# Two attention branches on one core: permuting the 16x16 weights instead of the evictions, and 744 instead of 712 score tiles on VectorE

## The chip, the core and the metric

The program runs on one core of one Trainium2 chip. The core has five engines with a queue each: TensorE (PE, matmuls), VectorE (DVE), ScalarE (ACT), GpSimd (POOL) and SyncE (SP, which only issues transfers here). PE writes into PSUM, eight banks of 128 partitions x 512 fp32; DVE and ACT read PSUM and write SBUF; POOL works in SBUF. The metric is the device time of one execution in microseconds, as the median of several runs.

## The reference

With S = 2048 rows, D = 512, H = 32 heads of 16 columns:

```python
def _A_ref(x, wqkv, w_phi, wo):
    q, k, v = ...                       # from x @ wqkv, per head
    pq = jnp.einsum("bhsd,hdf->bhsf", q, w_phi)
    pk = jnp.einsum("bhsd,hdf->bhsf", k, w_phi)
    phi_q = jnp.concatenate([_softmax(pq), _softmax(-pq)], axis=-1)
    phi_k = jnp.concatenate([_softmax(pk), _softmax(-pk)], axis=-1)
    kv, z = ...                         # sums over s of phi_k x v, and of phi_k
    o = num / den                       # phi_q x kv, phi_q x z
    return o.reshape(B, S, D) @ wo
def _B_ref(x, wqkv, wo):
    scores = jnp.einsum("bhqd,bhkd->bhqk", q, k) * (Dh ** -0.5)
    p = _softmax(scores, axis=-1)
    return (p @ v).reshape(B, S, D) @ wo
x = A_x
g = _sigmoid((x * gate_w).sum(-1, keepdims=True))
return g * _A_ref(...) + (1 - g) * _B_ref(...)
```

Branch A is linear attention with a learned feature map; branch B is ordinary softmax attention, and most of the work.

## The kernel before

**Branch B.** A block is one head out of each of four groups and one chunk of 512 queries; there are 32 blocks. A block has 64 score tiles of 128 keys x 512 queries (4 heads x 16 key tiles), 2,048 in all. A score matmul (`qk_mm`, L1290) contracts over 32 rows only, so matmuls of different heads run side by side in the rows of the PE array. Two tiles at a time go to ACT, which makes the exponential of 128 x 1024 from PSUM into `E_t` (L1381). Two such pairs of banks take turns, so the pair j+2 is written when ACT has read pair j. The remaining tiles of a block, `DN[b]` of them, go to DVE through three other banks: DVE adds a constant and writes int16 (L1367; L1357 where two tiles are joined in one instruction of 1,024 columns), which read as bf16 is a coarse exponential. POOL adds a constant to four int16 at a time in int64 words (L1343), into a second buffer and later once more on that buffer, for a group of four tiles; the three versions together approximate the exponential. The products with V (`pv_mm`, L1402) contract over 128 keys and give 32 columns, so four of them run side by side in the columns of the array. An ACT tile needs one product, a DVE tile three. The buffers of the DVE tiles (`Tx`, `Ty`, `Tz`, `oT`, `WoA`, `vA` and more) are borrowed from tensors not needed at the time.

**Branch A.** `Wp` is the projection folded with the 16x16 feature weights: for queries and for keys, `WAT` (the transposed projection) times a block-diagonal matrix `Wbd` of the 16x16 weights. Eight small DMAs on POOL's queue write the blocks of `Wbd` (L1039). `wp_fill` makes the eight products into PSUM (L1624, four matmuls of 128 columns each), and a DVE copy puts each into `Wp` (L1628). That copy also reorders the columns: four heads at a time, from head-major (j, f) to feature-major (f, j), which is a write with stride four. Later stages read `Wp` in that order (`phi`, L1051 for the matmuls).

**Fillers.** Where PE would have little to do, the planner puts matmuls with a tensor of zeros in (L1392).

**What sets the order.** All operations are declared with engine, duration, priority, reads and writes. `Plan.layout` schedules them in a list by modelled durations and gives an order for each engine. `settle` then changes that order by a table, `MOVES`: for each engine pairs (from, to) of places in its queue; `drop`, PE operations (fillers) that are left out; `banks`, another PSUM bank for a fill; `pairs`, two DVE tiles joined in one instruction; `locks`, POOL adds that are made to wait for a DVE operation. Every queue runs in the order that results, with semaphores for the dependencies. `DN` feeds `layout`: it says how many tiles of each block DVE takes, and so how many pairs ACT has.

Of the kernel before, what the change touches and what calls it, by code (L numbers as in the profile page):

```python
# [15 lines left out]
D = 512  # L16
H = 32
DH = 16
KT = 4
# [11 lines left out]
DN = (6, 20, 20, 24, 26, 22, 22, 20, 22, 22, 24, 18, 22, 20, 20, 26, 30, 22, 24, 26, 22, 24, 22, 26, 18, 22, 28, 18, 24, 24, 32, 16)  # L31
# [60 lines left out]
    ),  # L92
    "act": (
# [3 lines left out]
    ),  # L97
# [795 lines left out]
def _build(ctx, nc, A_x, A_wqkv, A_w_phi, A_wo, B_wqkv, B_wo, gate_w, out):  # L893
    names = [0]

    def sb(shape, dt=BF16, name="sb"):
        names[0] += 1
        return ctx.enter_context(nc.sbuf_tensor(f"{name}_t{names[0]}", shape, dt))
# [6 lines left out]
    WAT = sb([128, 8, D], name="WAT")  # L905
# [1022 lines left out]
```

## Time and profile before

| | us |
|---|---|
| runs, median of 3 | 682.58 (682.48 to 683.23) |
| profiled execution, its own time | 682.9 |
| its span, first to last instruction | 680.7 |
| ACT busy in it | 656.2 |
| PE busy in it | 670.5 |
| DVE busy in it | 591.1 |
| POOL busy in it | 383.2 |

The profile is of one execution. Busy is the time in which at least one instruction of the engine ran; a matmul's end is modelled, and neighbouring ones overlap, so PE's 670.5 is more than the time in which it could take no further work. A line of a group gives source line, engine, operation, tiles, shapes and count, then busy time in all, mean ns of one, and the idle time of the engine just before them with what ended it. In the timeline the first two columns are start and duration. In the windows each engine has its busy time and, in brackets, its number of instructions.

### The profile page before, as it was taken

Reading aid. Unit: us, or ns where it says so; the run is one execution under the profiler, and the core shown is the slowest. Engines: PE = TensorE matmul, PEld = TensorE weight load, DVE = VectorE, ACT = ScalarE, POOL = GpSimd, SP = SyncE. Lnnn points to the kernel's source line nnn. Section 1 sums busy time; section 2 is a strip of 40 time slices with the busy share of each in tenths; the row PEclk is TensorE's granted clock in tenths of the full one; section 3 lists DMA queues with packets and bytes.
Section 4 is the critical chain, followed back from the end, with each engine's and each line's share of the span. In section 5 each row is a group of like instructions: output and inputs, shape, how many; then the busy total and the mean of one; then the engine's idle time right before and its main releaser. Section 6 shows DMA issues by size and latency. Waiting matters only on the chain.

```text
span 680.7 us, 20896 instructions
## 1 busy us (share of the span) xinstructions
PE 670.5 (99%) x8995; PEld 232.9 (34%) x8995; DVE 591.1 (87%) x920; ACT 656.2 (96%) x739; POOL 383.2 (56%) x415
## 2 busy tenths in 40 slices
PE   8989999999999999999999999999999999999997
PEld 4322333334233333333233233322332333333333
DVE  4699889878998889898988989899799888989984
ACT  6999999999999999999999999999999999999995
POOL 7045466543666445654666766665656646565853
PEclk9999999999999999999999999999999999999999
DMA  6800100000010000000113022121321324033221
GB/s 132 161 29 10 29 16 15 19 14 19 10 23 15 11 18 11 17 18 14 18 41 87 27 69 72 46 49 48 81 66 34 68 72 99 27 72 82 65 72 39
DMA packets 67467, 30.95 MB, mean 45 GB/s; under 512 B 52696, under 2 KB 62296, under 8 KB 67376
## 3 DMA queue, kind: packets, MB, share of 16 engines
q1 hardware_dynamic: 66368, 28.95, 18.0%
q8 instruction: 70, 1.15, 0.7%
q10 hardware_dynamic: 576, 0.52, 0.2%
q0 software_dynamic: 432, 0.15, 0.1%
q14 instruction: 21, 0.17, 0.1%
HBM read 7.87 MB, written 8.88 MB: 25 GB/s over the span
## 4 chain that ended last, share of the span: by engine, by line
PE 78%; ACT 15%; DVE 5%; DMA 1%; issue 0%
PE psO L1402 28%; PE psS L1290 27%; PE psS L1051 15%; ACT E_t L1381 14%; PE psO L1392 2%; PE psS L1666 2%; DVE Wp_t L1628 1%; PE psS L1763 1%; DMA ld<-Tf_t 1%; PE psS L1142 1%; PE psS L1155 1%; PE psS L1750 1%; DVE Tz_t L1367 1%; DVE Ty_t L1357 1%; PE psS L1005 0%; DVE Tx_t L1367 0%
## 5 line engine op out<-in xcount | busy, mean ns | idle before, releaser
L1381 ACT ACTIVATE E_t<-psS 128x1024 bf16<-128x1024 f32 x668 | 625.2, 1054 | 12.9 <-PE psS L1290 11.6
L1290 PE MATMUL psS<-qz_t,kTB_t 32*128 32x512 bf16 x2048 | 275.4, 384 | 4.2 <-DVE Wp_t L1628 1.5
L1367 DVE TENSOR_SCALAR Tx_t<-psS 128x512 int16<-128x512 f32 x232 | 154.4, 685 | 15.5 <-PE psS L1290 14.0
L1290 PEld LDWEIGHTS psS<-qz_t,kTB_t 32*128 32x128 bf16 x2048 | 71.9, 91 | 236.3 <-ACT E_t L1381 114.6
L1402 PE MATMUL psO<-E_t,vaug_t 128*32 128x512 bf16 (+1 forms) x1336 | 109.4, 383 | 0.0
L1343 POOL INT64_ADD vA_t<-vA_t x69 | 68.0, 992 | 26.0 <-PE psO L1402 24.5
L1367 DVE TENSOR_SCALAR Ty_t<-psS 128x512 int16<-128x512 f32 x106 | 71.3, 684 | 8.8 <-PE psS L1290 7.6
L1402 PE MATMUL psO<-vA_t,vaug_t 128*32 128x512 bf16 x494 | 48.0, 383 | 0.0
L1367 DVE TENSOR_SCALAR oT_t<-psS 128x512 int16<-128x512 f32 x60 | 40.5, 683 | 5.5 <-PE psS L1290 4.9
L1367 DVE TENSOR_SCALAR Tz_t<-psS 128x512 int16<-128x512 f32 x58 | 39.0, 685 | 6.3 <-PE psS L1290 6.0
L1343 POOL INT64_ADD Ty_t<-Ty_t x39 | 39.8, 1019 | 7.5 <-PE psO L1402 7.4
L1343 POOL INT64_ADD Ty_t<-Tx_t x28 | 28.3, 1010 | 26.5 <-DVE Tx_t L1367 13.9
L1402 PE MATMUL psO<-Ty_t,vaug_t 128*32 128x512 bf16 (+1 forms) x414 | 41.6, 384 | 0.0
L1343 POOL INT64_ADD phiQT_t<-Tx_t x18 | 17.9, 992 | 41.0 <-DVE Tx_t L1367 34.6
L1367 DVE TENSOR_SCALAR vA_t<-psS 128x512 int16<-128x512 f32 x52 | 35.0, 684 | 6.3 <-PE psS L1290 6.3
L1402 PEld LDWEIGHTS psO<-E_t,vaug_t 128*32 128x32 bf16 (+1 forms) x1336 | 27.3, 95 | 38.2 <-issue 27.1
L1051 PE MATMUL psS<-xT_t,WB_t 128*32 128x512 bf16 x464 | 38.0, 383 | 0.1
L1051 PE MATMUL psS<-Wp_t,xT_t 128*32 128x512 bf16 x512 | 37.8, 382 | 0.0
L1367 DVE TENSOR_SCALAR WAT_t<-psS 128x512 int16<-128x512 f32 x50 | 33.5, 682 | 3.0 <-PE psS L1290 2.7
L1343 POOL INT64_ADD vA_t<-Tx_t x20 | 19.9, 998 | 25.8 <-DVE Tx_t L1367 24.6
L1367 DVE TENSOR_SCALAR Wp_t<-psS 128x512 int16<-128x512 f32 x46 | 31.0, 684 | 2.4 <-PE psS L1290 1.8
L1392 PE MATMUL psO<-xT_t,zero_t 128*32 128x512 bf16 x328 | 32.0, 385 | 0.0
(165 smaller groups left out, 914.3 us busy)
## 6 DMA issues: line engine op xcount, KB each, us to landing
dpq<-EA_t SPq DMA_DIRECT2D x16, 256.0 KB, 2.1
Rb_t<-lr SPq DMA_DIRECT2D x120, 32.0 KB, 1.8
dpo<-kv_t SPq DMA_DIRECT2D x16, 128.0 KB, 1.8
qz_t<-qz_t SPq DMA_DIRECT2D x120, 16.0 KB, 1.8
Tf_t<-Tf_t SPq DMA_DIRECT2D x60, 32.0 KB, 2.0
WB_t<-in_B_wqkv_dram SPq DMA_DIRECT2D x3, 384.0 KB, 4.4
out_dram<-WvA_t SPq DMA_DIRECT2D x8, 128.0 KB, 1.9
out_dram<-WB_t SPq DMA_DIRECT2D x6, 128.0 KB, 1.9
```

The costliest lines, as they stand in the source:

```text
L1051: ins = e.matmul(out[32 * i:32 * i + 32, :], lhsT=lhsT[:, 32 * i:32 * i + 32], rhs=rhs, start=start, stop=stop, tile_position=(0, 32 * i))
L1142: mms = [lambda e, ap, i=i, t=t: e.matmul(ap[:, 128 * i:128 * (i + 1)], lhsT=xT[:, t, NQ * c + 128 * i:NQ * c + 128 * (i + 1)], rhs=W_B[:, ...
L1155: mms = [lambda e, ap, i=i, t=t: e.matmul(ap[:, 256 * i:256 * (i + 1)], lhsT=xT[:, t, NQ * c + 128 * (2 * hf + i):NQ * c + 128 * (2 * hf + ...
L1290: return e.matmul(bank, lhsT=kT_B[32 * i:32 * i + 32, ROW[b // 2] % 2, 128 * kt:128 * (kt + 1)], rhs=qz[32 * i:32 * i + 32, b // 2 % 4, b ...
L1343: op = P.add("pool", P64 + W64 * size, d_prio(g["ts"][0]) - 5.0 + (0.0 if key == "s" else M_LATE), lambda e: e.int64_add(words(dst), words ...
L1357: return e.tensor_scalar(dst[:, a[0]:a[1] + 1:a[1] - a[0], :].bitcast(I16), src[:, b[0]:b[1] + 1:b[1] - b[0], :], EXPB, 0.0, op0=ALU.add, ...
L1367: ops.append(drain(f, mm, "dve", 0.70, d_prio(d), lambda e, ap, q=q: e.tensor_scalar(quarter(tb, q).bitcast(I16), ap, EXPB, 0.0, op0=ALU.a ...
L1381: op = P.add("act", EXP_OVH + 0.4267 * n, 0.0, lambda e: e.activation(Ebuf[:, j // 2 % EPAIRS, 512 * SZ[0] * (j % 2):512 * SZ[0] * (j % 2) ...
L1392: ins = e.matmul((psO if bank is None else bank)[32 * i:32 * i + 32, :], lhsT=zero[:], rhs=xT[:, 0, 0:NQ], start=bank is not None, stop=ba ...
L1402: return e.matmul(psO[32 * i:32 * i + w, :], lhsT=vaug[:, kt, o:o + w], rhs=rhs, start=start, stop=stop, tile_position=(0, 32 * i), skip_g ...
L1628: wp_ops.append(drain(f, mm, "dve", 0.69, prio, lambda e, ap: e.tensor_copy(Wp[:, t, D * qk:D * (qk + 1)].rearrange("p (a f j) -> p a j f" ...
L1666: mms = [lambda e, ap, n=n, f=f: e.matmul(ap[:, 64 * n:64 * n + 64].rearrange("p (s g j) -> p s g j", s=2, j=4), lhsT=ident[:], rhs=es[n][ ...
```

## The change

A second tensor `Wbp` holds the block-diagonal weights with their columns already in the feature-major order. One copy on POOL makes it from `Wbd` once the eight DMAs have landed. The products of `wp_fill` use `Wbp`, and the DVE copy behind them becomes plain. In six blocks more tiles go to DVE: four more in blocks 5, 6, 12 and 13, eight more in blocks 22 and 26.

```diff
-DN = (6, 20, 20, 24, 26, 22, 22, 20, 22, 22, 24, 18, 22, 20, 20, 26, 30, 22, 24, 26, 22, 24, 22, 26, 18, 22, 28, 18, 24, 24, 32, 16)
+DN = (6, 20, 20, 24, 26, 26, 26, 20, 22, 22, 24, 18, 26, 24, 20, 26, 30, 22, 24, 26, 22, 24, 30, 26, 18, 22, 36, 18, 24, 24, 32, 16)
...
 MOVES = {
...
     Wbd = sb([128, KT, 128], name="Wbd")
+    Wbp = sb([128, KT, 128], name="Wbp")
...
     P.join_writes(wbd_ops, "Wbd")
+    pool(1.0, -3.9, lambda e: e.tensor_copy(Wbp[:].rearrange("p r (a f j) -> p (r a) f j", f=DH, j=4),
+                                            Wbd[:].rearrange("p r (a j f) -> p (r a) f j", j=4, f=DH)),
+         reads=["Wbd"], writes=["Wbp"], name="wbp")
...
     def wp_fill(qk, t, prio):
         mms = [lambda e, ap, r=r: e.matmul(ap[:, 128 * r:128 * (r + 1)], lhsT=WAT[:, 4 * qk + r, 128 * t:128 * (t + 1)],
-                                           rhs=Wbd[:, r, :], start=True, stop=True) for r in range(KT)]
-        f, mm = fill(prio, mms, ["Wbd"] + [("WAT", 4 * qk + r) for r in range(KT)], name=f"W{qk}{t}", chunk=4,
+                                           rhs=Wbp[:, r, :], start=True, stop=True) for r in range(KT)]
+        f, mm = fill(prio, mms, ["Wbp"] + [("WAT", 4 * qk + r) for r in range(KT)], name=f"W{qk}{t}", chunk=4,
                      dur=0.07, cols=128)
-        wp_ops.append(drain(f, mm, "dve", 0.69, prio, lambda e, ap: e.tensor_copy(
-            Wp[:, t, D * qk:D * (qk + 1)].rearrange("p (a f j) -> p a j f", j=4, f=DH), ap.rearrange("p (a j f) -> p a j f", j=4, f=DH)),
+        wp_ops.append(drain(f, mm, "dve", 0.69, prio, lambda e, ap: e.tensor_copy(Wp[:, t, D * qk:D * (qk + 1)], ap),
                             writes=[("Wp", qk, t)], name=f"We{qk}{t}"))
```

The table `MOVES` is another throughout, on every engine. Its lists grow or shrink a little: places moved on PE 1,835 to 1,856, on DVE 569 to 584, on POOL 180 to 191, on SP 101 to 92, on ACT 33 both; banks 581 to 613, locks 187 to 204, joined pairs 54 both, dropped fillers 207 to 201.

Built, the two programs differ in their instructions as follows; everything else has the same count in both, in another order.

| engine | instruction | before | after |
|---|---|---|---|
| ACT | exponential of two tiles into `E_t` | 668 | 652 |
| DVE | score tiles (joined pairs counted twice) | 712 | 744 |
| DVE | strided copy into `Wp` | 8 | 0 |
| DVE | plain copy into `Wp` | 0 | 8 |
| POOL | copy `Wbd` to `Wbp` | 0 | 1 |
| POOL | int64 adds | 374 | 390 |
| PE | products with V from `E_t` | 1,336 | 1,304 |
| PE | products with V from DVE tiles | 2,136 | 2,232 |
| PE | fillers | 364 | 300 |
| PE | all matmuls | 8,995 | 8,995 |

663 rows, old and new, of the table MOVES are left out of this document.

## The prediction

> **What bounds the kernel now.** I read the page's busy times and chain first, then the groups by line, then the timeline of an ordinary stretch, then windows of 20 us for the places where that stretch is not typical.
>
> ```profile
> span 680.7 us, 20896 instructions
> PE 670.5 (99%) x8995; PEld 232.9 (34%) x8995; DVE 591.1 (87%) x920; ACT 656.2 (96%) x739; POOL 383.2 (56%) x415
> PE 78%; ACT 15%; DVE 5%; DMA 1%; issue 0%
> ...
> L1381 ACT ACTIVATE E_t<-psS 128x1024 bf16<-128x1024 f32 x668 | 625.2, 1054 | 12.9 <-PE psS L1290 11.6
> ...
> L1367 DVE TENSOR_SCALAR Tx_t<-psS 128x512 int16<-128x512 f32 x232 | 154.4, 685 | 15.5 <-PE psS L1290 14.0
> ```
>
> Two engines are nearly full at once. An exponential on ACT takes 625.2/668 = 0.936 us of its time, and ACT hardly idles before one (12.9 us in all). The chain of waits, however, runs through PE for 78% of the span. DVE has room, 591.1 of 680.7. A busy PE is not yet a PE at its limit, so the timeline has to say which of the two ends last:
>
> ```profile
> 299.65 6.55 ACT L1381 ACTIVATE E_t<-psS 128x1024 bf16<-128x1024 f32 x7
> ...
> 303.75 0.39 PE L1290 MATMUL psS<-qz_t,kTB_t 32*128 32x512 bf16 x3
> ...
> 304.07 0.40 PE L1402 MATMUL psO<-Tx_t,vaug_t 128*32 128x512 bf16 x4
> ...
> 304.30 0.39 PE L1402 MATMUL psO<-phiQT_t,vaug_t 128*32 128x512 bf16 x4
> ...
> 304.62 0.39 PE L1290 MATMUL psS<-qz_t,kTB_t 32*128 32x512 bf16 x3
> ```
>
> Matmuls on different strips of the array start together, as one pass. After a pass of the same tiling the next starts 0.23 us later (304.07 to 304.30); after a change between row tiling (scores) and column tiling (products with V) it starts 0.32 us later, so a change costs about 0.10 us more. One score pass and two column passes are 0.87 us, against 0.936 us for the exponential: ACT wins here by 0.07 us, and a third column pass would make PE last. Counted in the built program, PE's queue has 1,238 runs of one tiling, with 118 further row passes and 905 further column passes inside them: 1,238 x 0.32 + 1,023 x 0.23 = 631 us, before the short whole-array products. So PE is a second bound close behind ACT. The windows say how often each is last:
>
> ```profile
> 40.00:60.00 20.00, 17.55 (x187) 5.37 (x187) 20.00 (x24) 17.24 (x18) 10.27 (x10) 1.00 0.03 7
> ...
> 120.00:140.00 20.00, 20.00 (x298) 7.78 (x296) 16.27 (x24) 20.00 (x25) 10.20 (x12) 1.00 0.06 16
> ...
> 340.00:360.00 20.00, 19.98 (x299) 7.22 (x295) 17.17 (x30) 18.72 (x22) 12.47 (x13) 1.00 0.11 35
> ...
> 480.00:500.00 20.00, 20.00 (x290) 7.22 (x292) 16.57 (x29) 20.00 (x24) 11.97 (x13) 1.00 0.38 89
> 500.00:520.00 20.00, 19.86 (x264) 6.76 (x256) 19.42 (x32) 20.00 (x24) 13.04 (x14) 1.00 0.12 36
> ...
> 660.00:680.00 20.00, 17.01 (x262) 6.92 (x254) 10.50 (x18) 13.45 (x15) 7.20 (x7) 0.97 0.16 48
> sum 680.00, PE 670.50 PEld 232.91 DVE 591.10 ACT 656.20 POOL 383.21; mean PE 19.72 PEld 6.85 DVE 17.39 ACT 19.30 POOL 11.27
> ```
>
> Columns after the length are PE, PE loads, DVE, ACT, POOL, clock. ACT is busy for 20.00 of 20 in 15 of the 34 windows (as at 120 and 480), and short of it in the rest (as at 340). The window at 40 alone has DVE full and ACT down at 17.24.
>
> **The change part by part.**
>
> *Sixteen exponentials less.* Tiles on DVE go from 712 to 744, so ACT makes 652 exponentials: 16 x 0.936 = 15.0 us less on ACT. That is the gain if ACT ends every stretch.
>
> *PE.* Per tile moved, one product leaves and three come: 96 - 32 = 64 matmuls more; 64 filler matmuls (a product with zeros) go. PE's total stays what it was. Counted by passes: score passes 725 to 723, column passes 1,436 to 1,437, runs 1,238 to 1,203. With the prices above, -1 x 0.23 - 35 x 0.10 = -3.7 us. That is the gain if PE ends every stretch.
>
> I weigh the two by the windows: 15/34 x 15.0 + 19/34 x 3.7 = 8.7 us. Both ends stay for the range.
>
> *The evictions of Wp.* Eight strided writes become plain ones:
>
> ```profile
> L1628 DVE CAST Wp_t<-psS 128x512 bf16<-128x512 f32 x8 | 10.2, 1298 | 0.0
> ...
> L1118 DVE CAST kTB_t<-psS 128x512 bf16<-128x512 f32 x14 | 9.6, 686 | 3.6 <-PE psS L1051 3.4
> ```
>
> ```profile
> L1628 DVE CAST Wp_t<-psS x8: 1278/1296/1325, 39.7 to 57.1; 128x512 bf16<-128x512 f32 x8
> ```
>
> ```profile
> 42.22 0.38 PE L1290 MATMUL psS<-qz_t,kTB_t 32*128 32x512 bf16 x1 [0.72 <-DVE Wp_t L1628]
> ...
> 43.51 1.02 ACT L1381 ACTIVATE E_t<-psS 128x1024 bf16<-128x1024 f32 x1 [0.87 <-PE psS L1290]
> ```
>
> The plain form of the same shape, L1118, takes 0.686 us against 1.298: 8 x 0.61 = 4.9 us off DVE, all between 39.7 and 58.4 us. There it is on the path: the score matmul at 42.22 stands behind an eviction, and the exponential at 43.51 stands behind the matmul. ACT lost 20 - 17.24 = 2.8 us in that window. At most that comes back, at least nothing; since the new order puts further DVE tiles close by, I take 1.0.
>
> *The copy on POOL.* No row has a 128x512 copy; its neighbours are these:
>
> ```profile
> 2.43 2.29 POOL L1030 MEMSET vaug_t<- 128x512 bf16 x1
> ...
> 9.16 4.09 POOL L1039 DMA_DIRECT2D Wbd_t<-in_A_w_phi_dram  x8 [0.17 <-POOL mask_t L1043]
> 13.24 0.25 POOL L1044 COPY mask_t<-mask_t 128x64 bf16<-128x64 bf16 x1
> 30.73 0.61 POOL L1343 INT64_ADD phiQT_t<-Tx_t  x1 [17.24 <-DVE Tx_t L1367]
> ```
>
> ```profile
> L1624 PE MATMUL psS<-Wbd_t,WAT_t x32: 219/219/230, 38.7 to 56.4; 128*128 128x128 bf16 x32
> ...
> DMA to landing us min/median/max: 2.3/2.6/3.6
> ```
>
> A strided fill of that size took 2.29 us, an eighth of the copy 0.25 (times eight, 2.0); from below, the small copy's 0.25 is a floor. I take 2.0. It is a new wait at the head of POOL's queue: eight landings, the last issued by 13.25 and landed by 16.9 at the latest. Queued behind it are the adds, the first at 30.73 after 17.24 us of idleness, and the Wp products on PE from 38.7. That idleness covers it: nothing. With the cover gone it would be 2.0 us on the first add and, through it, on the first products.
>
> *DVE.* Thirty-two tiles at 154.4/232 = 0.666 us are 21.3, less 4.9: 16.4 us more, 607.5 in all. Against a span near 670 that is 91%, so in total it fits. It need not fit in every place. Block 22 and block 26 get eight more tiles each, and in the built order, cut into stretches of 24 exponentials, tiles on DVE per stretch had two values above 31 (33 and 32) and now have five (36, 34, 34, 32, 32). Other DVE work is (591.1 - 712 x 0.666)/28 = 4.2 us a stretch, and a stretch lasts 680.7/668 x 24 = 24.5 us. DVE is over that by 3.7 us at 36 tiles, 2.3 at 34, 1.0 at 32: 10.3 in sum, against 2.7 before. Neighbouring stretches have room, but only three banks hold scores ahead of DVE. Bounds 0 and +7.6; I take half, 3.8.
>
> *POOL.* Sixteen more adds:
>
> ```profile
> L1343 POOL INT64_ADD vA_t<-vA_t x69 | 68.0, 992 | 26.0 <-PE psO L1402 24.5
> ```
>
> ```profile
> L1512 DVE TENSOR_TENSOR oT_t<-Tf_t,Rb_t x15: 627/682/691, 83.9 to 656.2; 128x512 bf16<-128x512 f32 x15
> ```
>
> At 0.99 each that is 15.8 us on an engine that is 56% busy: about 399 + 2 of some 670. It waits mostly for PE to free a buffer, so it is not last: nothing. The order's list also ties 204 adds to a DVE operation instead of 187; such a wait holds POOL's queue alone. SP issues the same 501 transfers in another order: nothing. These two hide behind the same exponentials; uncovered, one add is worth at most its own 1.0 us.
>
> DVE's multiplies with two SBUF inputs (L1512) took at most 0.691 us, no more than a plain eviction, so none of the 15 stood behind an add. The Trainium skill (SBUF — State Buffer, "SBUF: two separate sides") has it that such an operation and a GpSimd instruction that reads SBUF exclude each other for a whole instruction; by that rule 17 more POOL instructions can cost up to 17 us where they meet, and the trace agrees only in that it shows no meeting.
>
> **Sum.** 682.9 is the profiled execution's own time (span 680.7 and 2.2 around it). -8.7 - 1.0 + 3.8 = -5.9: 677.0. That execution is 0.3 above the median of the runs, 682.58, so I forecast **676.7**.
>
> **The rivals.**
>
> *ACT ends everything.* If the new order fits PE's work and DVE's crowded places under the exponentials, the full 15.0 comes, and up to 2.8 in the Wp stretch: 682.6 - 15.0 - 2.0 = 665.6. For it: the cycle at 303.75 has ACT last by 0.07 us. Against it: 19 windows where ACT is not full.
>
> *PE ends everything.* -3.7 + 3.8 leaves 682.6, no change. For it: 631 us of passes and changes, and the chain's 78%. Against it: 300 of 364 filler matmuls are still in the built program, and a stretch with fillers has room on PE.
>
> *DVE takes the bound in the crowded stretches.* There DVE drains the banks late, the next score matmul waits for one, and what stands behind it on PE, ACT's next pair among it, waits too, as at 42.22. ACT's saving is then idle time. Place: the five stretches above; price: the full 7.6, with PE last elsewhere (-3.7) and nothing from Wp: 682.6 + 3.9 = **686.5**, slower. It decides once a stretch holds more than (24.5 - 4.2)/0.666 = 30.5 tiles. For it: the window at 40, where full DVE cost ACT 2.8 us. Against it: the window at 500, where DVE had 19.42 and ACT still 20.00.
>
> *A POOL add meets a two-input DVE operation*, and one of the two stands for 0.99 us. If half of the 17 new POOL instructions did, and PE or ACT stood with it, 8.4 us would be added: 685.1. It is the rule cited above that makes this possible.
>
> *The clock falls.* In the last window PE is at 17.01 of 20 and its clock at 0.97. With 64 fillers gone a stretch might thin out like that; at 0.97 over half the span, 10 us more: 686.7. But the fillers are replaced one for one, in less time. The Trainium skill (TensorE: Matmul & The Clock Gate, "What's actually happening") has the clock fall after an idle window of some 3.4 us; the trace has no such hole in PE before the tail.
>
> *The plain eviction is not plain*, and stays at 1.30 us: the 1.0 and half of the 4.9 are lost, 680.2. L1118 speaks against it.
>
> **How the numbers follow.** Forecast 0.47 (670 to 681); ACT ends everything 0.19; PE ends everything 0.08; DVE crowded 0.19; port 0.03; clock 0.02; eviction not plain 0.02. A difference under about 0.2%, or 1.4 us, can't be told from none here. Faster by more than that: 0.47 + 0.19 + 0.02 = 0.68; within it 0.08; slower 0.24. The range 666 to 688 takes in all bounds but the corners: below it half of the second case lies, above it some of the slower ones.
>
> **What would show it.** ACTIVATE to E_t x652 at an unchanged 0.936 (busy by count), and ACT's idle time before it between 13 and 25 us: right; 30 or more, with waits of the score loads on DVE tiles doubled: DVE crowded. Evictions of Wp near 0.69 us and the window 40 to 60 with ACT above 18.5: that step right. The copy between 16 and 20 us, and no Wp product waiting for it. Granted clock 1.00 outside the tail. The forecast is wrong if ACT's busy time falls by 15 us and the span by less than 2 or by more than 13.

## The result, and the profile after

| | before | after |
|---|---|---|
| median of the runs, us | 682.88 (682.48 to 683.23) | 676.08 (675.27 to 676.94) |
| profiled execution, us | 682.9 | 675.81 |
| its span, us | 680.7 | 673.9 |

The ratio of the times is 0.9901, with an interval of 0.9884 to 0.9918: 6.8 us faster, where 5.9 were forecast. The page of the changed kernel, in lines that answer to those of before (busy times, chain, the exponentials; the second half of the kernel has moved down by 10 or 11 lines):

```profile
PE 665.2 (99%) x8995; PEld 233.7 (35%) x8995; DVE 602.8 (89%) x952; ACT 643.0 (95%) x723; POOL 401.0 (59%) x432
...
PE 81%; DVE 9%; ACT 7%; DMA 1%; issue 1%; SPq 0%; DVEq 0%
...
L1392 ACT ACTIVATE E_t<-psS 128x1024 bf16<-128x1024 f32 x652 | 611.6, 1049 | 20.0 <-PE psS L1301 16.1
```

ACT lost 13.2 us of work (656.2 to 643.0), the span half of that. PE lost 5.3, and ACT's part of the chain went from 15% to 7%. An exponential still takes 0.94 us of ACT (611.6/652).

The first thing to look for is where on the way the 6.8 us appear. From the trace, the time at which the first exponential of a block starts:

| block | tiles added | before | after | difference |
|---|---|---|---|---|
| 1 | 0 | 35.1 | 34.8 | -0.3 |
| 2 | 0 | 58.9 | 55.3 | -3.6 |
| 4 | 0 | 101.2 | 96.5 | -4.7 |
| 7 | 4 each in 5 and 6 | 164.6 | 157.9 | -6.7 |
| 8 | 0 | 185.1 | 179.4 | -5.8 |
| 22 | 8 in it | 471.5 | 464.6 | -6.9 |
| 23 | 0 | 493.1 | 482.7 | -10.4 |
| 24 | 0 | 511.5 | 504.1 | -7.4 |
| 26 | 8 in it | 553.0 | 545.8 | -7.2 |
| 27 | 0 | 571.9 | 562.0 | -9.9 |
| 28 | 0 | 595.2 | 588.6 | -6.6 |
| end | | 680.7 | 673.9 | -6.7 |

At the start of block 5, the first that got more tiles, 5.2 us are there (120.6 to 115.5), three quarters. Blocks 22 and 26, with sixteen of the 32 new tiles, gain some 3 us each while they run, for want of exponentials, and the block behind each gives it back.

The first stretch is that of the `Wp` evictions. The timeline of ACT in it, before and then after (start, duration, what ran; in brackets the idle time ahead and what ended it):

```profile
33.21 9.43 ACT L1381 ACTIVATE E_t<-psS 128x1024 bf16<-128x1024 f32 x10
43.51 1.94 ACT L1381 ACTIVATE E_t<-psS 128x1024 bf16<-128x1024 f32 x2 [0.87 <-PE psS L1290]
45.67 3.27 ACT L1381 ACTIVATE E_t<-psS 128x1024 bf16<-128x1024 f32 x3 [0.22 <-PE psS L1290]
49.13 1.94 ACT L1381 ACTIVATE E_t<-psS 128x1024 bf16<-128x1024 f32 x2 [0.20 <-PE psS L1290]
51.53 4.69 ACT L1381 ACTIVATE E_t<-psS 128x1024 bf16<-128x1024 f32 x5 [0.46 <-PE psS L1290]
56.93 2.98 ACT L1381 ACTIVATE E_t<-psS 128x1024 bf16<-128x1024 f32 x3 [0.71 <-PE psS L1290]
```

```profile
32.97 28.03 ACT L1392 ACTIVATE E_t<-psS 128x1024 bf16<-128x1024 f32 x30
```

Before, 25 exponentials took from 33.21 to 59.91, 1.07 us each. After, 30 of them ran without a break in 28.03, 0.934 each. At that pace 25 take 23.4 us, so 3.3 us were lost before. The gaps add up to only 2.46: the rest lies in the short rows between them, since two exponentials in a row take 1.94, 0.97 each, and 0.93 is only reached in a long row. Records of neighbours overlap there, so a break costs more than the gap that the timeline shows. This is why counting idle time undersells the loss. The evictions and the new copy, in the views by tile and of POOL's timeline:

```profile
L1639 DVE CAST Wp_t<-psS x8: 677/680/692, 35.1 to 51.9; 128x512 bf16<-128x512 f32 x8
```

```profile
L1635 PE MATMUL psS<-Wbp_t,WAT_t x32: 219/219/230, 34.4 to 51.4; 128*128 128x128 bf16 x32
```

```profile
16.97 1.08 POOL L1050 COPY Wbp_t<-Wbd_t 128x512 bf16<-128x512 bf16 x1 [3.52 <-DMA Wbd_t<-in_A_w_phi_dram]
33.23 0.61 POOL L1354 INT64_ADD phiQT_t<-Tx_t  x1 [15.18 <-DVE Tx_t L1378]
```

An eviction is 0.680 us (median of eight). The copy takes 1.08 us behind the landings, POOL then idles for 15.18, and the first product that reads it comes at 34.4: it is hidden. Last, windows of 20 us (PE, PE loads, DVE, ACT, POOL, clock), one in the `Wp` stretch, two in the crowded blocks and the tail:

```profile
40.00:60.00 20.00, 20.00 (x244) 6.28 (x242) 19.45 (x28) 19.91 (x23) 12.33 (x12) 1.00 0.03 7
480.00:500.00 20.00, 19.91 (x300) 7.58 (x300) 19.41 (x35) 17.45 (x22) 13.82 (x14) 1.00 0.25 66
560.00:580.00 20.00, 19.74 (x278) 6.99 (x270) 20.00 (x34) 15.93 (x17) 14.15 (x15) 1.00 0.28 76
660.00:680.00 20.00, 10.49 (x174) 4.66 (x166) 5.86 (x10) 7.11 (x9) 4.14 (x4) 0.93 0.08 27
```

In the first, PE went from 17.55 to 20.00 and ACT from 17.24 to 19.91. In the third, DVE is full and ACT idles for 4 us, as in the first before the change; that looks like DVE as the bound, and the third experiment below tests it.

### The profile page after: what moved, and what is told of

Read it like the earlier page. It is cut to its first block, busy times and chain, and to the rows that moved or that the text cites. A ratio compares the mean times of both kernels' runs of the same rounds, so it can differ in the third digit from the quotient of the medians.

```text
span 673.9 us, 20931 instructions
## 1 busy us (share of the span) xinstructions
PE 665.2 (99%) x8995; PEld 233.7 (35%) x8995; DVE 602.8 (89%) x952; ACT 643.0 (95%) x723; POOL 401.0 (59%) x432
## 4 chain that ended last, share of the span: by engine, by line
PE 81%; DVE 9%; ACT 7%; DMA 1%; issue 1%; SPq 0%; DVEq 0%
PE psS L1301 29%; PE psO L1413 28%; PE psS L1062 14%; ACT E_t L1392 6%; PE psS L1676 3%; DVE Tx_t L1378 2%; PE psO L1403 2%; DVE Ty_t L1378 1%; PE psS L1153 1%; PE psS L1166 1%; DVE WAT_t L1378 1%; DMA ld<-Tf_t 1%; PE psS L1773 1%; DMA Lq_t<-ld 1%; DVE vA_t L1378 1%
## 5 line engine op out<-in xcount | busy, mean ns | idle before, releaser
L1392 ACT ACTIVATE E_t<-psS 128x1024 bf16<-128x1024 f32 x652 | 611.6, 1049 | 20.0 <-PE psS L1301 16.1
L1378 DVE TENSOR_SCALAR Tx_t<-psS 128x512 int16<-128x512 f32 x250 | 164.3, 681 | 13.2 <-PE psS L1301 11.8
L1413 PE MATMUL psO<-E_t,vaug_t 128*32 128x512 bf16 (+1 forms) x1304 | 106.4, 383 | 0.1
L1354 POOL INT64_ADD vA_t<-vA_t x72 | 71.5, 1001 | 35.7 <-PE psO L1413 21.3
L1354 POOL INT64_ADD Ty_t<-Ty_t x42 | 43.3, 1032 | 15.0 <-PE psO L1413 10.2
L1413 PE MATMUL psO<-vA_t,vaug_t 128*32 128x512 bf16 (+1 forms) x520 | 49.9, 383 | 0.0
L1413 PE MATMUL psO<-Ty_t,vaug_t 128*32 128x512 bf16 x436 | 43.9, 383 | 0.0
L1378 DVE TENSOR_SCALAR WAT_t<-psS 128x512 int16<-128x512 f32 x58 | 39.2, 685 | 4.2 <-PE psS L1301 3.8
L1378 DVE TENSOR_SCALAR oT_t<-psS 128x512 int16<-128x512 f32 x56 | 37.4, 683 | 5.1 <-PE psS L1301 4.8
L1413 PEld LDWEIGHTS psO<-E_t,vaug_t 128*32 128x32 bf16 (+1 forms) x1304 | 27.4, 95 | 35.3 <-issue 22.5
L1062 PE MATMUL psS<-Wp_t,xT_t 128*32 128x512 bf16 x512 | 37.7, 382 | 0.0
L1378 DVE TENSOR_SCALAR vA_t<-psS 128x512 int16<-128x512 f32 x52 | 35.1, 683 | 2.4 <-PE psS L1301 1.9
L1062 PE MATMUL psS<-xT_t,WB_t 128*32 128x512 bf16 x464 | 36.6, 383 | 0.0
L1413 PE MATMUL psO<-Tx_t,vaug_t 128*32 128x512 bf16 x282 | 29.7, 387 | 0.0
```

What stands on the lines that cost most here:

```text
L1062: ins = e.matmul(out[32 * i:32 * i + 32, :], lhsT=lhsT[:, 32 * i:32 * i + 32], rhs=rhs, start=start, stop=stop, tile_position=(0, 32 * i))
L1354: op = P.add("pool", P64 + W64 * size, d_prio(g["ts"][0]) - 5.0 + (0.0 if key == "s" else M_LATE), lambda e: e.int64_add(words(dst), words ...
L1378: ops.append(drain(f, mm, "dve", 0.70, d_prio(d), lambda e, ap, q=q: e.tensor_scalar(quarter(tb, q).bitcast(I16), ap, EXPB, 0.0, op0=ALU.a ...
L1392: op = P.add("act", EXP_OVH + 0.4267 * n, 0.0, lambda e: e.activation(Ebuf[:, j // 2 % EPAIRS, 512 * SZ[0] * (j % 2):512 * SZ[0] * (j % 2) ...
L1413: return e.matmul(psO[32 * i:32 * i + w, :], lhsT=vaug[:, kt, o:o + w], rhs=rhs, start=start, stop=stop, tile_position=(0, 32 * i), skip_g ...
```

## The experiments

They begin with the two parts of the change, apart (1, 2). Then DVE is made shorter where it is crowded (3) and where it is not (4), ACT everywhere (5, 6), and PE in its fillers (7). Another home for DVE's work follows (8), then a shorter PE (9, 10), and then two and three engines shorter at once (11, 12). Each was run beside the kernel before; ratios are to that. Differences to the changed kernel are to the 676.08 of the result above, since it wasn't run again; the kernel before came to between 682.84 and 683.02 in these later runs.

**1. The plain evictions alone, in the old order.**

```diff
+    Wbp = sb([128, KT, 128], name="Wbp")
...
-                                           rhs=Wbd[:, r, :], start=True, stop=True) for r in range(KT)]
+                                           rhs=Wbp[:, r, :], start=True, stop=True) for r in range(KT)]
...
-            Wp[:, t, D * qk:D * (qk + 1)].rearrange("p (a f j) -> p a j f", j=4, f=DH), ap.rearrange("p (a j f) -> p a j f", j=4, f=DH)),
+        wp_ops.append(drain(f, mm, "dve", 0.69, prio, lambda e, ap: e.tensor_copy(Wp[:, t, D * qk:D * (qk + 1)], ap),
...
+    q.insert(max(k for k, o in enumerate(q) if o.name.startswith("wbd") or o.name == "mk2") + 1, wbp)
```

> The kernel before with its own order and 712 tiles; only the weights are permuted by the POOL copy and the eight evictions of Wp are plain. Theory A (the plain evictions are worth most of the gain, since DVE was last between 39 and 58 us): 4 to 5 us faster than before, about 678.3; window 40 to 60 with ACT above 19.5. Theory B (the prediction's size for this step, the rest of the early gain being the new order): about 1 us faster, 681.8. Theory C (nothing of it shows in the end, later stretches absorb it): 682.8.

Measured: 678.51 against 682.96, ratio 0.9925 (0.9897 to 0.9952), 4.45 us faster. ACT's timeline of this run:

```profile
33.21 26.95 ACT L1397 ACTIVATE E_t<-psS 128x1024 bf16<-128x1024 f32 x29
```

The order is that of before; only eight evictions and the copy differ, and the gaps are gone: 29 exponentials in 26.95, and ACT is busy for all 20.00 us from 40 to 60. By this run the plain evictions are worth about two thirds of the gain. The run's interval and the changed kernel's overlap, so the other third is not shown by it alone.

**2. The new tiles and the new order, with strided evictions.** The copy stays in, and nothing reads it.

```diff
-                                           rhs=Wbp[:, r, :], start=True, stop=True) for r in range(KT)]
+                                           rhs=Wbd[:, r, :], start=True, stop=True) for r in range(KT)]
...
-        wp_ops.append(drain(f, mm, "dve", 0.69, prio, lambda e, ap: e.tensor_copy(Wp[:, t, D * qk:D * (qk + 1)], ap),
+        wp_ops.append(drain(f, mm, "dve", 0.69, prio, lambda e, ap: e.tensor_copy(
+            Wp[:, t, D * qk:D * (qk + 1)].rearrange("p (a f j) -> p a j f", j=4, f=DH), ap.rearrange("p (a j f) -> p a j f", j=4, f=DH)),
```

> The changed kernel with its new order and 744 tiles; the evictions of Wp are strided again (1.30 us) and the products use the unpermuted weights; the copy on POOL is still made and unused. Theory A: 4 to 5 us slower than the changed kernel, about 680.5, that is 2 us faster than before, which would be the worth of the moved tiles and the new order. Theory B: about 1 us slower, 677.

Measured: 679.4, ratio 0.9951 (0.9929 to 0.9973): 3.3 us above the changed kernel's 676.08, and 3.6 below before. The view by tile and the window at 40:

```profile
L1639 DVE CAST Wp_t<-psS x8: 1285/1317/1342, 35.4 to 55.2; 128x512 bf16<-128x512 f32 x8
```

```profile
40.00:60.00 20.00, 18.34 (x205) 5.63 (x203) 19.98 (x24) 17.80 (x20) 10.50 (x11) 1.00 0.03 8
```

The holes in PE and ACT are back. So the evictions bring 3.3 us (by this run) to 4.45 (by the first), and tiles and order the remaining 2.4 to 3.6.

Tiles and order were not run apart, but the traces divide them in part. Block 5, the first with more tiles, starts at 120.6 before, at 116.7 with the evictions alone, at 119.2 with the order and the tiles alone, and at 115.5 with all. Up to there no tile has moved: the evictions bring 3.8 to 3.9 and the new order 1.3 to 1.4. Of the 6.7 us in the end, 1.5 are left for the 32 tiles and the rest of the order.

The traces can also be cut into stretches of 24 exponentials. In us, from the first exponential of a stretch to the first of the next:

| stretch | before | 1 | after | 2 | 3 |
|---|---|---|---|---|---|
| 1 | 24.7 | 22.0 | 22.3 | 25.6 | 22.4 |
| 2 | 24.1 | 22.8 | 22.2 | 22.5 | 22.2 |
| 7 | 22.2 | 22.2 | 22.2 | 22.2 | 22.2 |
| 19 | 24.0 | 24.0 | 26.6 | 26.7 | 26.4 |
| 22 | 23.0 | 23.0 | 26.1 | 26.2 | 25.9 |
| 23 | 24.1 | 24.2 | 27.0 | 27.0 | 26.8 |

**3. DVE's tiles at half their columns, where DVE is crowded** (stretches 19, 20, 22, 23).

```diff
+            c = 256 if g["n"] in HALF else 512
-            return e.tensor_scalar(dst[:, a[0]:a[1] + 1:a[1] - a[0], :].bitcast(I16), src[:, b[0]:b[1] + 1:b[1] - b[0], :], EXPB, 0.0,
+            return e.tensor_scalar(dst[:, a[0]:a[1] + 1:a[1] - a[0], 0:c].bitcast(I16), src[:, b[0]:b[1] + 1:b[1] - b[0], 0:c], EXPB, 0.0,
...
+        if op.kind == "dq" and (pairs - 1) // 24 in (19, 20, 22, 23):
+            share[op.group] += 1
```

> The changed kernel; about 136 DVE tiles, those whose scores are made between the exponentials 456 to 503 and 528 to 575, are evicted by half (256 of 512 columns), so the output is not the reference's. This takes some 0.3 us each off DVE in the stretches where it was full after the change. Theory D (DVE took the bound there, the gain of the tiles moved into blocks 22 and 26 was lost in it): 4 to 6 us faster than the changed kernel, about 671, and ACT's idle time before the exponentials down from 20 to about 12. Theory P (PE ends these stretches): under 1.5 us faster.

Measured: 676.03, ratio 0.9885 (0.9839 to 0.9932): the changed kernel's time. A window of this run:

```profile
560.00:580.00 20.00, 19.65 (x278) 6.61 (x272) 14.42 (x34) 16.41 (x18) 15.55 (x16) 1.00 0.31 76
```

DVE falls from 20.00 to 14.42 in it, and ACT has only one instruction more in it. The account called D, that DVE is the bound there, falls, although DVE was full and ACT idle.

**4. The same where DVE has room**, by `in (7, 8, 9, 16, 17)` in place of the four stretches of the third.

> The changed kernel; about the same number of DVE tiles (148) are evicted by half, but those of the exponentials 168 to 239 and 384 to 431, where DVE had idle time. Theory D: 0 to 1.5 us faster, since DVE is not last there. If it gains as much as the run with the crowded tiles, DVE matters everywhere alike and crowding is no cause.

Measured: 675.3, ratio 0.9874 (0.9834 to 0.9914), 0.8 below the changed kernel, whose ratio the interval holds. In neither set of stretches does a shorter DVE alone bring a gain that is clear of noise; at the `Wp` evictions, in the first experiment, it did.

**5 and 6. Shorter exponentials**, in the changed kernel and in the kernel before: 960 of 1,024 columns from the 60th on.

```diff
-            Ebuf[:, j // 2 % EPAIRS, 512 * SZ[0] * (j % 2):512 * SZ[0] * (j % 2) + 512 * n], psS[:, 512 * base:512 * (base + n)], ACTF.Exp, scale=ESCALE),
+            Ebuf[:, j // 2 % EPAIRS, 512 * SZ[0] * (j % 2):512 * SZ[0] * (j % 2) + 512 * n - 64 * (j >= 60)],
+            psS[:, 512 * base:512 * (base + n) - 64 * (j >= 60)], ACTF.Exp, scale=ESCALE),
```

> The changed kernel; every exponential from the 60th on makes 960 of its 1,024 columns (592 of them, some 0.055 us each, 33 us of ACT in all); the output is not the reference's. If ACT ended every stretch, some 30 us faster. If it ended the share of windows that the prediction weighed (15 of 34), some 14. If PE and DVE stand right behind it, under 6.

> The kernel before with the same cut (608 exponentials, some 33 us of ACT). By the prediction's weights some 14 us faster; if PE stands right behind ACT, under 6; ACT all alone, 30. It should gain more here than in the changed kernel, if the change used up part of what ACT held.

Measured: 675.06, ratio 0.9876 (0.982 to 0.9932), 1.0 below the changed kernel, whose ratio the interval holds; and 680.94, ratio 0.9965 (0.9944 to 0.9987), 2.1 below before. The groups of the exponential, first of the changed kernel with this edit, then of before with it:

```profile
L1392 ACT ACTIVATE E_t<-psS 128x960 bf16<-128x960 f32 (+1 forms) x652 | 590.3, 982 | 35.3 <-PE psS L1301 25.8
```

```profile
L1381 ACT ACTIVATE E_t<-psS 128x960 bf16<-128x960 f32 (+1 forms) x668 | 604.5, 981 | 28.3 <-PE psS L1290 19.0
```

The exponentials are 21.3 us shorter in the one (611.6 to 590.3) and 20.7 in the other (625.2 to 604.5). Idle time took three quarters of it (20.0 to 35.3, and 12.9 to 28.3). In the kernel before, then, ACT passed on a tenth of what it saved; counted by the fall of the recorded duration, 73 ns for each of some 600, it would be less still.

**7. No fillers in the products' bank.** 66 passes with zeros, 264 matmuls, are left out of PE's queue.

```diff
+    idle = [o for o in P.order["pe"] if o.name == "idle" and o.acq is None]
...
+    P.order["pe"] = [o for o in P.order["pe"] if o not in idle]
+    for op in zero_ops.values():
+        op.extra = 0
```

> The changed kernel without its 264 filler products into the output bank (66 passes, 14 us of PE's time). If fillers stand only where PE has room: within 1 us of the changed kernel, clock 1.00. If PE is last where they stand: 3 us faster or more. If they hold the clock up: slower, with a granted clock under 1.00.

Measured: 674.66, ratio 0.9868 (0.9821 to 0.9914), 1.4 below the changed kernel. The interval holds the changed kernel's ratio, so a gain isn't shown: of 14 us of PE's time, 1.4 came through, if any. The fillers stand mostly where PE would wait anyway.

**8. Seven of DVE's other evictions on ACT**, near the crowded places.

```diff
+    for name, j in (('Ke3.0', 335), ('Ke3.2', 337), ('Ke3.3', 341), ('Oe2', 480), ('Oe5', 549), ('Oe6', 552), ('ev.26', 560)):
+        op = next(o for o in P.order["dve"] if o.name == name)
+        P.order["dve"].remove(op)
+        P.order["act"].insert(P.order["act"].index(exp_ops[j]), op)
```

> The changed kernel with seven evictions (three of the keys, three of output tiles, one of the output bank) given from DVE to ACT, in the stretches where DVE was full and ACT idle. Computes what the reference does. Theory D: each takes 0.6 us off a full DVE; 1.5 to 3.5 us faster than the changed kernel, about 673.5. Theory P: no change, or slower by what ACT takes on, up to 3 us.

Measured: 676.93, ratio 0.9903 (0.9873 to 0.9933), 0.85 above the changed kernel, whose ratio the interval holds: neither a gain nor a cost is shown, and the 1.5 to 3.5 us of the account called D did not come.

**9 and 10. Shorter products with V**, in the changed kernel and in the kernel before: 448 of 512 columns from block 4 on, in 751 passes.

```diff
-        return e.matmul(psO[32 * i:32 * i + w, :], lhsT=vaug[:, kt, o:o + w], rhs=rhs, start=start,
+        c = 448 if b >= 4 and not start else 512
+        return e.matmul(psO[32 * i:32 * i + w, 0:c], lhsT=vaug[:, kt, o:o + w], rhs=rhs[:, 0:c], start=start,
```

> The changed kernel; from block 4 on, all products with V but the first of each head and block stream 448 of 512 columns (3,005 matmuls, some 751 passes, 0.027 us each: 20 us of PE's time); the output is not the reference's. Theory P (PE's own pace of passes and tiling changes ends nearly every stretch, in both kernels): 10 to 17 us faster than the changed kernel, until ACT, busy 643 of 674, stands behind it. If PE only follows ACT and DVE: under 3 us.

> The kernel before with the same cut (2,941 matmuls, 20 us of PE's time). Theory P: faster by less than the changed kernel gains, since ACT is nearer here (656 us busy): 7 to 12 us. If PE only follows: under 3 us.

Measured: 671.62, ratio 0.9831 (0.9814 to 0.9847), 4.5 below the changed kernel; and 679.26, ratio 0.9946 (0.9931 to 0.9961), 3.8 below before. What the edit takes from PE is read in the groups kept apart by shape, of the kernel before with it:

```profile
L1403 PE MATMUL psO<-E_t,vaug_t 128*32 128x448 bf16 x1027 | 78.8, 356 | 0.0
...
L1403 PE MATMUL psO<-E_t,vaug_t 128*32 128x512 bf16 x297 | 27.8, 384 | 0.0
```

A product is 28 ns shorter, so 751 passes (735 in the kernel before) are 21 us. PE, in the chain for 78%, passed on a fifth. Both results lie between the ranges of the two accounts, so neither of these holds as it stands.

**11. Both at once**, in the changed kernel: the edits of the fifth and the ninth.

> The changed kernel with the products cut as in e9 and, besides, the exponentials from the 60th on at 960 of 1,024 columns. Theory P: ACT no longer stands behind PE, so the whole 20 us of PE's time come, 16 to 20 us faster than the changed kernel, while the cut of the exponentials alone gave 1 us. If it is no faster than e9, DVE or the waits between the engines are next.

Measured: 665.17, ratio 0.9754 (0.9731 to 0.9778), 10.9 below the changed kernel. Alone they brought 1.0 and 4.5. The 16 to 20 us of the account called P did not come.

**12. All three**: with that, DVE's tiles from block 8 on at 448 of 512 columns.

```diff
-                quarter(tb, q).bitcast(I16), ap, EXPB, 0.0, op0=ALU.add, op1=ALU.max),
+                quarter(tb, q)[:, 0:c].bitcast(I16), ap[:, 0:c], EXPB, 0.0, op0=ALU.add, op1=ALU.max),
```

> The changed kernel with the products and the exponentials cut as in e11 and, besides, the 576 DVE tiles of blocks 8 to 31 evicted over 448 of 512 columns (some 0.06 us each, 35 us of DVE); the output is not the reference's. Theory L (PE, ACT and DVE wait for each other in a loop through the score banks, so that each cut alone is worth little and all together much): 5 to 10 us faster than e11, about 657, though the crowded tiles cut alone gave nothing. Theory P' (what is left after e11 is PE's own order and the waits of blocks on each other): under 2 us faster than e11.

Measured: 656.48, ratio 0.9605 (0.958 to 0.9629), 19.6 below the changed kernel and 8.7 below the eleventh. The busy times of the eleventh, then of the twelfth:

```profile
PE 652.5 (98%) x8995; PEld 234.7 (35%) x8995; DVE 599.4 (90%) x952; ACT 621.0 (94%) x723; POOL 400.1 (60%) x432
```

```profile
PE 646.0 (99%) x8995; PEld 233.0 (36%) x8995; DVE 573.3 (88%) x952; ACT 616.4 (94%) x723; POOL 400.1 (61%) x432
```

DVE gave up 26.1 us, and 8.7 came through, where 30 us less of it in the crowded stretches (602.8 to 572.6 in the third) had brought nothing. With about 20 us taken off each of PE and ACT and 26 off DVE, the time fell by about what PE gave up. This is what the account called L foretold: a saving on one engine ends for the most part in a wait for another, and only a saving on all three comes through whole. Why is argued and not shown. PE, ACT and DVE hand score banks to each other in one fixed order, which is L's reason; three engines that each need almost the whole time, without a loop between them, would give the same numbers.

## Why the prediction was right, and what in it was wrong

The time was right by two errors that cancel, which is luck. The forecast sum was -8.7 - 1.0 + 3.8; measured are -2.4 to -3.6 for the first and third terms together (forecast: -4.9), of which 1.3 to 1.4 fall before the first block with more tiles, and -3.3 to -4.5 for the second.

**Sixteen exponentials less, weighed with PE: -8.7. Wrong in the weights.** A window in which ACT is busy for 20.00 was counted as one in which ACT ends last. The sixth and tenth runs measure the weights on the kernel before: 2.1/20.7 = 0.10 for ACT, where 15/34 = 0.44 was used, and 3.8/21 = 0.18 for PE, where 19/34 = 0.56 was. They don't add up to one, since the rest comes only when several engines are cut together. With these, 15.0 x 0.10 + 3.7 x 0.18 = 2.2 us, an estimate near the lower measured end. It is not the only reading, since a weight from a cut of 21 us need not hold for the first 3.7. PE is busy for 20.00 in 15 of the 34 windows too, and from 60 to 650 us the steps from one PE pass to the next, counted in the trace, exceed the median of their kind (0.23 and 0.32) by only some 18 us in all before, and 20 after. So PE's 3.7 us in full, as in the rival "PE ends everything", fit the measured 2.4 to 3.6 about as well; with the measured evictions and without the crowding term that rival gives 674.5 to 675.6, close to 676.08. The 0.936 us an exponential held as busy time by count, and so did ACT's idle time: 20.0, within the 13 to 25 named.

**The evictions of Wp: -1.0 within 0 to -2.8. Mis-sized, and the bound was too narrow.** Duration and place were right. The bound took ACT's idle time in one window for all that could be lost. But 25 exponentials at 1.07 us instead of 0.93 had lost 3.3, and counted by stretches the loss is 4.0: in the first experiment stretch 1 is 2.7 shorter and stretch 2, in which the last eviction lies, 1.3. The row that should have counted was in the prediction: at 40 to 60 DVE was full and PE, the chain's engine, had 17.55 of 20. Of the windows quoted it was the only one before the tail where PE had a hole of more than 0.2 us, and DVE was full; there the whole 4.9 us off DVE were open to come through, and 3.3 to 4.45 did. The forecast also feared that new tiles close by would use up the room; the blocks up to 4 got none.

**DVE crowding: +3.8. The place was right, the mechanism was not.** The stretches 19, 22 and 23 did become longer, by 2.6, 3.1 and 2.9 us, and hold 6, 2 and 5 more score tiles for the same 24 exponentials. Blocks 22 and 26 came out even: with the block behind each they take 39.5 and 42.8 us, and 40.0 and 42.2 before. But half-length tiles on DVE left the stretches within 0.2 us. Shorter exponentials (26.6, 26.0 and 27.0) and no fillers (26.7, 26.2 and 27.7) didn't help them either, and with all three engines shorter they took 25.6, 24.9 and 25.7. For 19 and 22 the trace names PE itself. Counted by the starts of its matmuls, PE has 95 and 96 passes there, where it had 86 and 83; 41 and 38 steps between them change the tiling; there are 32 short matmuls of the whole array in each, and no filler. At 0.23 and 0.32 us a pass and 0.03 for a short matmul that is 26.5 us for each (an estimate), of 26.6 and 26.1 measured. Only part of the added work is that of the moved tiles: stretch 19 has 10 products with V more, 12 matmuls of projections and feature maps (L1062) and 16 short ones; stretch 22 has 4, 48 and 32 more. The new order put work of PE there, and PE had no room for it. In stretch 23, with seven filler passes and DVE busy for 26.7 of 27.0 us, what holds it isn't settled. Moving fewer tiles into these two blocks needs another order and wasn't tried.

**The waits** show the same: fewer score loads wait for an exponential, a few more for a DVE tile (before: 114.6 us in 291 waits, and 16.3 in 43 for the tiles in `Tx`; for all DVE tiles together 54.2 before and 61.1 after). After:

```profile
PEld psS L1301 <- ACT E_t L1392: 100.7, 256, 0.7
...
PEld psS L1301 <- DVE Tx_t L1378: 18.4, 48, 0.5
```

The doubling of the DVE waits that would have shown DVE as the bound isn't there.

**Right:** the copy's cover, though not its size (1.08 us, within 0.25 to 2.29, taken 2.0); the plain eviction; the sixteen adds on POOL, busy for 401.0 without a trace on the path; SP's order. The rival of the port fell with them: DVE's fifteen multiplies with two SBUF inputs took at most 0.691 us, as before, with 17 more POOL instructions beside them. In the trace before none of the fifteen overlaps a POOL instruction, after the change six do, by at most 0.15 us; the kernel marks these multiplies and the adds with `lock`, and `layout` plans them apart. So the rule cited from the Trainium skill (SBUF — State Buffer, "SBUF: two separate sides") had next to nothing to act on here. The granted clock was 1.00 in the windows above and 0.93 only in the tail, where PE is busy for 10.49 of 20.

## What to carry to other kernels

When three engines are each busy for over 85% and hand buffers to each other in a fixed order, neither a full window nor an idle neighbour says what a saving is worth: shorten one engine, then two, then all, and see what comes through. Look for the places where the engine at the head of the chain has holes, since there a saving on the engine that makes the holes comes through nearly whole; here 4.9 us off DVE in such a place were worth about as much as 15 us off ACT spread over the rest together with a new order, or more. Measure a stall there by the pace of the work (1.07 against 0.93 us an exponential) and not by idle time alone.

## What the runs showed of the hardware

A DVE copy of 128x512 from PSUM that writes bf16 with a stride of four elements took 1.298 us in the kernel before and 1.317 in the second experiment, against 0.680 plain. The same permutation as a read of 128x512 bf16 from SBUF on POOL took 1.08 us. Exponentials of 128x1024 follow each other 0.905 us apart at the median in both traces, and never less than 0.904, though each is recorded with 1.05; so a row that is broken costs about 0.15 us at each break beyond the idle time shown, and a wait shorter than that doesn't show as idle time at all. The 0.93 and 0.936 used above hold some such waits. And the program repeats itself closely: of the 27 stretches of 24 exponentials, 23 in the first experiment are within 0.1 us of those of the kernel before, in another execution; the others are the two of the `Wp` evictions and two with 0.3 and 0.5.
